# Attention sink weights: turned in two halves on VectorE and through DRAM instead of on TensorE, with the values of two head pairs multiplied in mid-attention

## The chip, the cores and the metric

The kernel runs on one NeuronCore of one Trainium2 chip. The metric is the device time of one execution in microseconds (us). Three executions were timed, and one more was profiled. In the profile PE is the matrix engine (TensorE) and PEld its weight loads; DVE is VectorE, ACT is ScalarE, POOL is GpSimd, and SP is the engine whose queue issues most transfers here.

## The reference

A banded attention with sink keys feeds a two-layer feed-forward network with a PReLU in the middle. The shapes are batch 4, 8 heads, 768 positions, head size 64, a window of 128 keys, 4 sink keys; then 3072 rows, model width 512, inner width 2048.

```python
scores = scale * np.matmul(q, k.transpose(0, 1, 3, 2))
is_sink = pos[None, :] < int(n_sink)
in_window = (rel >= 0) & (rel < int(window))
scores = np.where(is_sink | in_window, scores, -1000000000.0)
a = np.exp(scores - np.max(scores, axis=-1, keepdims=True))
a = a / (np.sum(a, axis=-1, keepdims=True) + 1e-09)
attn_out = np.matmul(a, v)
x = attn_out.transpose(0, 2, 1, 3).reshape(B * S, H * D)
h = x @ w_in
g = np.maximum(h, 0.0) + alpha * np.minimum(h, 0.0)
out = g @ w_out
```

## The kernel before

The 3072 rows are worked in 12 chunks of 256 positions (`NCHUNK`), three to each batch. The attention of chunk c+1 runs beside the feed-forward network of chunk c. The network of a chunk has 16 slots (`NF`), one for each block of 128 inner columns: `gemm1` (12 matmuls, 256 columns wide), then the PReLU on ACT and DVE with a split into a high and a low part, and two slots later `gemm2` (6 matmuls, 512 columns wide, in two pieces). All products of the network are made from such high and low parts.

The attention of a chunk from 2 on takes 8 heads one after another. For each head and each half of the 256 positions there is a pair of score matmuls (L591, L592), the mask and the row minimum on DVE (L604), the exponential on ACT (L608). `finish_head` makes the reciprocals on DVE (L637, L638), the scaled weights of the window (L649, into a tile named comb), and on POOL the scaled weights of the four sink keys (L653, into the tile sink). The weights must then be turned, so that keys lie on partitions. From chunk 3 on (`PAIRED`) the window's weights of each head pair go this way in `swap`: DVE turns 32 by 32 blocks (L713), SP sends the tile to a DRAM scratch named swap (L716), and four transfers bring it back with the blocks in their turned places (L719). In `swapped` DVE multiplies them by triangles into a tile named wa (L730). The sink weights of all heads of a chunk are handled once, in `sink_step`: two DVE instructions split them into a high and a low part (L678, L679, tile ts), two PE transposes turn them (L684), and ACT copies them to sinkT (L687). `av_two` takes two head pairs at a time. It opens two PSUM banks with a matmul each of the sink weights (L816), adds the window's values (24 narrow matmuls at L746), and ACT and DVE split the result into xh and xl (L826, L827), which `gemm1` of the next chunk reads.

The order is not that of the code. A planner (`Plan.draw`) simulates the five engines with a cost for each operation and a rule for transfers, and picks at every point the operation that can start, by its rank. PE's operations are ranked in the order in which the program creates them, those of the others just ahead of the first that needs them. What the planner drew is then issued in that order on each engine, with real semaphore waits. `attention` gives the steps of a chunk as a list, and `spread` deals the 26 steps out over 12 of the 16 slots. In the planner a PE operation may start 0.5 us after an input from another engine is due:

```python
SLACK = 0.5
...
dma = max(dma, t + 1.5) + o.nbytes / 290e3
end = dma + 0.5
```

Tiles come from small pools: comb has 4, swap 2, sinkT 1, the PSUM kind pa 2, stage (raw queries and keys) 2, v 2.

Of the kernel before, what the change touches and what calls it, by code (L numbers as in the profile page):

```python
# [9 lines left out]
F32 = mybir.dt.float32  # L10
# [9 lines left out]
P = 128  # L20
# [300 lines left out]
def program(ctx, tc, qk, pairs, vp, vs, w, par, out):  # L321
# [12 lines left out]
    def several(name, n, shape, dtype):  # L334
        plan.kind(name, [pool.tile(shape, dtype, name=f"{name}{i}") for i in range(n)])

    scratch = ctx.enter_context(tc.tile_pool(name="scratch", bufs=1, space=bass.MemoryType.DRAM))
    plan.kind("swap", [scratch.tile([4, P, P], F32, name=f"swap{i}") for i in range(2)])
    several("stage", 2, [P, QC + KC], F32)
    several("kq", 2, [P, KC + 2 * QC], F32R)  # L340
    several("v", 2, [P, 3, 2, D], F32)
# [318 lines left out]

    def sink_step(c, g=0):
        sm, sk = sums[c], sink[c]
        heads = range(4 * g, 4 * g + 4) if c in SPLIT else range(H)
        if c in SPLIT:
            r, wide = val("ri"), val("ob")
            rinv[c, g] = wide
            four = lambda: r.at.rearrange("p (h u) -> p h u", u=2)
            op("DVE", 0.15, lambda: nc.vector.tensor_scalar(four(), sm.at[:, 4 * g:4 * g + 4], 1e-9, None, op0=ALU.add),
               reads=[(sm, (h, u)) for h in heads for u in range(2)], writes=[r])
            op("DVE", 0.16, lambda: nc.vector.reciprocal(four(), four()), writes=[r])  # L670
            each = lambda: r.at.rearrange("p (h u) -> p u h", u=2).unsqueeze(3).broadcast_to([P, 2, 4, D])
            fold = lambda: wide.at.rearrange("p (u h d) -> p u h d", u=2, h=4)
            op("ACT", cast(8 * D), lambda: nc.scalar.copy(fold(), each()), reads=[r], writes=[wide],
               other=("DVE", dve(8 * D, True), lambda: nc.vector.tensor_copy(fold(), each())))
        sp = lambda: sk.at.rearrange("p u h s -> p u (h s)").unsqueeze(2).broadcast_to([P, 2, 2, 32])
        ts, tp = val("ts"), val("pa")
        done = [(sk, h) for h in range(heads[-1] + 1)]
        op("DVE", 0.14, lambda: nc.vector.tensor_copy(ts.at[:, :, 0::2], sp()), reads=done, writes=[(ts, 0)])  # L678
        op("DVE", 0.2, lambda: nc.vector.tensor_tensor(ts.at[:, :, 1::2], sp(), ts.at[:, :, 0::2].bitcast(F32), ALU.subtract),  # L679
           reads=done + [(ts, 0)], writes=[(ts, 1)])  # L680

        def turn():
            for u in range(2):
                nc.tensor.transpose(tp.at[:, u * P:(u + 1) * P], ts.at[:, u].rearrange("p a x -> p (a x)").bitcast(F32), ident)  # L684
        op("PE", 2 * TURN, turn, reads=[ts], writes=[tp], tail=T_TAIL)
        st = sinkT[c] = val("sinkT")
        op("ACT", cast(QC, True), lambda: nc.scalar.copy(st.at, tp.at[:, :QC]), reads=[tp], writes=[st])  # L687
# [120 lines left out]
    def av_two(c, p):  # L808
        both = (p, p + 1)
        src, v = [wt.pop((c, x)) for x in both], [vtile.pop((c, x)) for x in both]  # L810
        bks = [val("pa") for _ in both]
        vt, st = vst[c // CPB], sinkT[c]

        def sinks():
            for bk, x in zip(bks, both):
                nc.tensor.matmul(bk.at[:, :QC], vt.at[:, x * P:(x + 1) * P], st.at, start=True, stop=False)  # L816
        op("PE", 2 * mm(QC), sinks, reads=[vt, st], writes=bks, tail=R_TAIL)
        x1, x2 = begin_x(c, p)

        def both_values():  # L820
            for n in range(2):
                values(c, v[n].at, lambda j: src[n].at.bitcast(F32)[:, j * 4 * P:(j + 1) * 4 * P], bks[n].at[:, :QC])
        op("PE", 2 * values_cost(c), both_values, reads=src + v, writes=bks, tail=N_TAIL, mode="col")
        for n, x in enumerate(both):
            a = bks[n]
            op("ACT", cast(QC, True), lambda a=a, x=x: nc.scalar.copy(x1.at[:, x], a.at[:, :QC]), reads=[a], writes=[(x1, x)])  # L826
            op("DVE", dve(QC), lambda a=a, x=x: nc.vector.tensor_tensor(x2.at[:, x], a.at[:, :QC], x1.at[:, x].bitcast(F32), ALU.subtract),  # L827
               reads=[a, (x1, x)], writes=[(x2, x)])
            if p + 2 < KT:
                load_v(c, x + 2)  # L830
# [65 lines left out]
    def attention(c):  # L896
        def a_step(h, u):
            def run():
# [5 lines left out]
                unit(c, h, u)  # L904
                if u == 1:
                    finish_head(c, h)
                    if h in (5, 6):
                        load_v(c, h - 5)
            return run

        def b_steps(pairs):
# [6 lines left out]
        if c in SPLIT:  # L918
# [16 lines left out]
                steps.insert(at, st)  # L935
            return steps
        steps = [a_step(h, u) for h in range(H) for u in range(2)]
        steps += [None, sk]
        if c >= PAIRED:
            for p in (0, 2):  # L940
                steps += [lambda p=p: trans(c, p), lambda p=p: trans(c, p + 1), None, lambda p=p: av_two(c, p)]
            return steps
        b = b_steps(range(KT))
        for n, st in enumerate(b):
            steps.append(st)
# [272 lines left out]
```

## Time and profile before

| quantity | value |
| --- | --- |
| median of the three timed executions | 679.52 us (679.45 to 680.26) |
| time of the profiled execution | 680.06 us |
| its span from the first to the last instruction | 678.4 us |
| PE busy in the span | 665.8 us (98%) |
| DVE busy | 522.7 us (77%) |
| ACT busy | 407.2 us (60%) |
| POOL busy | 31.7 us (5%) |
| mean granted TensorE clock | 0.997 of full speed |

The span leaves out what lies around the instructions. Matmuls are pipelined, so the duration of one in the trace is longer than the step to the next, and what a matmul costs PE is read from one start to the next start.

### The profile page before, as it was taken

The numbers are of one execution on the slowest core, as the hardware profiler recorded it, in microseconds if no ns is written. First come the engines' busy times: TensorE is split into PE (matmuls) and PEld (weight loads), VectorE is DVE, ScalarE is ACT, GpSimd is POOL, SyncE is SP. The second block draws the span as 40 slices with busy tenths as digits, with TensorE's granted clock in tenths as the row PEclk, the third lists the DMA queues.
The fourth block names the chain that finished last, engine by engine and source line by source line (L and its number), as shares of the span: only waits on it lengthen the run. The fifth ranks groups of instructions, "written<-read, shape, count | busy, mean of one in ns | idle before, by whom it ended". The sixth has DMA issues, their size and how long they took to land.

```text
span 678.4 us, 13475 instructions
## 1 busy us (share of the span) xinstructions
PE 665.8 (98%) x4552; PEld 582.2 (86%) x4552; DVE 522.7 (77%) x1759; ACT 407.2 (60%) x1093; POOL 31.7 (5%) x115
## 2 busy tenths in 40 slices
PE   9989999999999999999999999999999999999996
PEld 4568898988889989988988988988988988988995
DVE  6999999967967976976885985985895994895331
ACT  6989987837627636736735735744753852852432
POOL 2110000001000000010000000000000000000000
PEclk9989999999999999999999999999999999999999
DMA  8765541325342533443442542542442443322001
GB/s 312 270 217 212 189 164 46 120 79 149 102 118 91 142 106 115 136 126 95 126 141 77 143 125 82 155 134 71 137 119 81 143 115 104 115 74 71 32 2 36
DMA packets 67901, 82.60 MB, mean 122 GB/s; under 512 B 5872, under 2 KB 48880, under 8 KB 67824
## 3 DMA queue, kind: packets, MB, share of 16 engines
q1 hardware_dynamic: 64272, 68.55, 34.1%
q10 hardware_dynamic: 3552, 13.11, 5.6%
q8 instruction: 38, 0.62, 0.4%
q14 instruction: 39, 0.32, 0.1%
HBM read 65.91 MB, written 15.73 MB: 120 GB/s over the span
## 4 chain that ended last, share of the span: by engine, by line
PE 82%; DVE 9%; ACT 5%; issue 1%; DMA 1%; POOL 0%; SPq 0%; ACTq 0%; DVEq 0%
PE bank L841 34%; PE bank L878 12%; PE bank L876 11%; PE bank L879 11%; PE bank L746 5%; PE bank L591 3%; PE bank L592 3%; DVE wa L393 2%; DVE w L401 2%; ACT pt L608 1%; ACT wa L379 1%; DVE wa L391 1%; DVE gl L848 1%; PE bank L1031 1%; DVE g L846 1%
## 5 line engine op out<-in xcount | busy, mean ns | idle before, releaser
L841 PE MATMUL bank<-xh,w 128*128 128x256 f32 x1536 | 307.7, 281 | 1.7 <-DVE g L846 1.5
L841 PEld LDWEIGHTS bank<-xh,w 128*128 128x128 f32 x1536 | 251.0, 189 | 10.6 <-DVE g L846 3.4
L841 PE MATMUL bank<-xl,w 128*128 128x256 f32 x768 | 214.8, 280 | 0.0
L845 ACT ACTIVATE g<-bank,param 128x256 f32<-128x256 f32 x192 | 90.5, 473 | 131.4 <-PE bank L841 128.8
L878 PE MATMUL bank<-w,gh 128*128 128x512 f32 x382 | 153.1, 401 | 0.0
L879 PE MATMUL bank<-w,gh 128*128 128x512 f32 x382 | 149.9, 392 | 0.0
L841 PEld LDWEIGHTS bank<-xl,w 128*128 128x128 f32 x768 | 145.2, 189 | 5.3
L846 DVE TENSOR_TENSOR g<-bank,g 128x256 f32<-128x256 f32 x192 | 80.1, 419 | 58.2 <-ACT g L845 57.4
L876 PE MATMUL bank<-w,gl 128*128 128x512 f32 x382 | 119.9, 395 | 0.0
L847 ACT CAST gh<-g 128x256 fp32r<-128x256 f32 x192 | 77.1, 404 | 66.8 <-DVE g L846 65.8
L608 ACT ACTIVATE pt<-pt,nm 128x260 f32<-128x260 f32 (+1 forms) x192 | 94.0, 490 | 17.7 <-DVE nm L604 17.1
L848 DVE TENSOR_TENSOR gl<-g,gh 128x256 fp32r<-128x256 f32 x192 | 81.1, 424 | 30.2 <-ACT gh L847 27.6
L876 PEld LDWEIGHTS bank<-w,gl 128*128 128x128 f32 x382 | 69.7, 188 | 14.5 <-issue 0.7
L604 DVE CUSTOM_DVE_ANT_0 pt<-bank,masks 128x260 f32<-128x260 f32 (+1 forms) x192 | 73.9, 400 | 8.5 <-PE bank L592 5.5
L878 PEld LDWEIGHTS bank<-w,gh 128*128 128x128 f32 x382 | 71.9, 188 | 9.9 <-issue 1.5
L879 PEld LDWEIGHTS bank<-w,gh 128*128 128x128 f32 x382 | 71.9, 188 | 8.3
L730 DVE TENSOR_TENSOR wa<-comb,tri 128x256 f32<-128x256 f32 x144 | 52.4, 419 | 12.4 <-DMA comb<-swap 12.2
L557 DVE TENSOR_TENSOR kq<-stage,kq 64x392 fp32r<-64x392 f32 x80 | 45.3, 566 | 10.7 <-ACT kq L555 8.7
L555 ACT CAST kq<-stage 128x392 fp32r<-128x392 f32 x80 | 41.5, 519 | 10.6 <-PE bank L592 7.3
L592 PE MATMUL bank<-kq 128*128 128x260 f32 (+1 forms) x160 | 44.5, 281 | 0.0
L591 PE MATMUL bank<-kq 128*128 128x260 f32 (+1 forms) x160 | 44.0, 279 | 0.1
L649 DVE CUSTOM_DVE_ANT_0 comb<-pt,ri 128x128 f32<-128x128 f32 x136 | 43.1, 346 | 0.0
(125 smaller groups left out, 657.4 us busy)
## 6 DMA issues: line engine op xcount, KB each, us to landing
stage<-qk SPq DMA_DIRECT2D x80, 324.0 KB, 2.9
wraw<-w ACTq DMA_DIRECT2D x12, 1024.0 KB, 5.2
swap<-comb SPq DMA_DIRECT2D x36, 256.0 KB, 2.2
comb<-swap SPq DMA_DIRECT2D x144, 64.0 KB, 2.1
v<-vp SPq DMA_DIRECT2D x44, 192.0 KB, 2.9
out_dram<-ob SPq DMA_DIRECT2D x22, 256.0 KB, 2.2
wraw<-w SPq DMA_DIRECT2D x4, 1024.0 KB, 11.3
lent<-pairs SPq DMA_DIRECT2D x4, 324.0 KB, 4.5
```

The source lines that it names most:

```text
L591: nc.tensor.matmul(s[:, w0], qh()[:, qs], ks()[:, kw], start=True, stop=False)
L592: nc.tensor.matmul(s[:, w0], ql()[:, qs], ks()[:, kw], start=False, stop=True)
L604: op("DVE", dve(n), lambda: nc.vector.tensor_tensor_reduce(out=pt.at[:, u, w0], in0=s.at[:, w0], in1=masks[:, i, w0], scale=-0.125, scalar ...
L608: op("ACT", exp(n), lambda: nc.scalar.activation(pt.at[:, u, w0], pt.at[:, u, w0], AF.Exp, bias=nm.at[:, h, u:u + 1], scale=-1.0, accum_ou ...
L841: nc.tensor.matmul(h(), fin.at[:, 0, part, ks], rhs.at[:, kt], start=(kt == 0 and n == 0), stop=(kt == KT - 1 and n == 2))
L845: op("ACT", act(QC, True), lambda: nc.scalar.activation(g.at, h(), AF.Copy, scale=alt[:, f:f + 1]), reads=[bk, known("param")], writes=[g])
L846: op("DVE", dve(QC), lambda: nc.vector.tensor_tensor(g.at, h(), g.at, ALU.max), reads=[bk], writes=[g])
L847: op("ACT", cast(QC), lambda: nc.scalar.copy(gh.at, g.at), reads=[g], writes=[gh])
L848: op("DVE", dve(QC), lambda: nc.vector.tensor_tensor(gl.at, g.at, gh.at.bitcast(F32), ALU.subtract), reads=[g, gh], writes=[gl])
L876: nc.tensor.matmul(o2[j].at, gl.at[:, js], fin.at[:, 1, 0], start=False, stop=(f == NF - 1))
L878: nc.tensor.matmul(o2[j].at, gh.at[:, js], fin.at[:, 1, 0], start=(f == 0), stop=False)
L879: nc.tensor.matmul(o2[j].at, gh.at[:, js], fin.at[:, 1, 1], start=False, stop=False)
```

## The change

For chunks 3 to 11 `sink_step` now runs twice, for heads 0 to 3 and for heads 4 to 7. Each time both DVE instructions handle the columns of all heads as before. In place of the two PE transposes and the ACT copy, DVE turns 32 by 32 blocks into a comb tile (L686 of the new file), SP sends them to a DRAM scratch named turns (L688), and four transfers bring them to sinkT (L691). The blocks in sinkT lie in another order, and the matmuls of the sink weights (L831) read them through a view with runs of 32 elements. The steps of `attention` are put in another order: the first half of the sink weights after head 3, the first two head pairs' values a few steps later, and heads 4 to 7 around and after them. The loads of v for pairs 0 and 1 are issued after heads 1 and 2 in place of 5 and 6.

```diff
--- before.py
+++ after.py
@@ -336,6 +336,7 @@
 
     scratch = ctx.enter_context(tc.tile_pool(name="scratch", bufs=1, space=bass.MemoryType.DRAM))
     plan.kind("swap", [scratch.tile([4, P, P], F32, name=f"swap{i}") for i in range(2)])
+    plan.kind("turns", [scratch.tile([4, P, 2 * 32], F32, name=f"turns{i}") for i in range(2)])
     several("stage", 2, [P, QC + KC], F32)
     several("kq", 2, [P, KC + 2 * QC], F32R)
     several("v", 2, [P, 3, 2, D], F32)
@@ -660,7 +661,7 @@
 
     def sink_step(c, g=0):
         sm, sk = sums[c], sink[c]
-        heads = range(4 * g, 4 * g + 4) if c in SPLIT else range(H)
+        heads = range(4 * g, 4 * g + 4) if c in SPLIT or c >= PAIRED else range(H)
         if c in SPLIT:
             r, wide = val("ri"), val("ob")
             rinv[c, g] = wide
@@ -673,11 +674,25 @@
             op("ACT", cast(8 * D), lambda: nc.scalar.copy(fold(), each()), reads=[r], writes=[wide],
                other=("DVE", dve(8 * D, True), lambda: nc.vector.tensor_copy(fold(), each())))
         sp = lambda: sk.at.rearrange("p u h s -> p u (h s)").unsqueeze(2).broadcast_to([P, 2, 2, 32])
-        ts, tp = val("ts"), val("pa")
+        ts = val("ts")
         done = [(sk, h) for h in range(heads[-1] + 1)]
         op("DVE", 0.14, lambda: nc.vector.tensor_copy(ts.at[:, :, 0::2], sp()), reads=done, writes=[(ts, 0)])
         op("DVE", 0.2, lambda: nc.vector.tensor_tensor(ts.at[:, :, 1::2], sp(), ts.at[:, :, 0::2].bitcast(F32), ALU.subtract),
            reads=done + [(ts, 0)], writes=[(ts, 1)])
+
+        if c >= PAIRED:
+            small, d = val("comb"), val("turns")
+            st = sinkT[c] = val("sinkT")
+            op("DVE", dve(QC), lambda: nc.vector.transpose(
+                small.at[:, :QC].rearrange("p (j u b) -> p u j b", u=2, j=4), ts.at.bitcast(F32)), reads=[ts], writes=[small])
+            op("SP", ISSUE, lambda: nc.sync.dma_start(d.at.rearrange("j p x -> p j x"), small.at[:, :QC].rearrange("p (j x) -> p j x", j=4)),
+               reads=[small], writes=[d], nbytes=4 * P * QC)
+            for j in range(4):
+                op("SP", ISSUE, lambda j=j: nc.sync.dma_start(
+                    st.at[j * 32:(j + 1) * 32].bitcast(F32).rearrange("a (i x) -> a i x", i=4), d.at[j].rearrange("(i a) x -> a i x", i=4)),
+                   reads=[d], writes=[(st, j)], nbytes=4 * 32 * QC)
+            return
+        tp = val("pa")
 
         def turn():
             for u in range(2):
@@ -813,7 +828,7 @@
 
         def sinks():
             for bk, x in zip(bks, both):
-                nc.tensor.matmul(bk.at[:, :QC], vt.at[:, x * P:(x + 1) * P], st.at, start=True, stop=False)
+                nc.tensor.matmul(bk.at[:, :QC], vt.at[:, x * P:(x + 1) * P], st.at.rearrange("p (i u b) -> p u i b", u=2, i=4), start=True, stop=False)
         op("PE", 2 * mm(QC), sinks, reads=[vt, st], writes=bks, tail=R_TAIL)
         x1, x2 = begin_x(c, p)
 
@@ -904,8 +919,9 @@
                 unit(c, h, u)
                 if u == 1:
                     finish_head(c, h)
-                    if h in (5, 6):
-                        load_v(c, h - 5)
+                    first = 1 if c >= PAIRED else 5
+                    if h in (first, first + 1):
+                        load_v(c, h - first)
             return run
 
         def b_steps(pairs):
@@ -935,11 +951,12 @@
                 steps.insert(at, st)
             return steps
         steps = [a_step(h, u) for h in range(H) for u in range(2)]
+        if c >= PAIRED:
+            for p, n in ((2, 16), (0, 8)):
+                steps[n:n] = [lambda p=p: sk(p // 2)]
+                steps[n + 3:n + 3] = [lambda p=p: trans(c, p), lambda p=p: trans(c, p + 1), None, lambda p=p: av_two(c, p)]
+            return steps
         steps += [None, sk]
-        if c >= PAIRED:
-            for p in (0, 2):
-                steps += [lambda p=p: trans(c, p), lambda p=p: trans(c, p + 1), None, lambda p=p: av_two(c, p)]
-            return steps
         b = b_steps(range(KT))
         for n, st in enumerate(b):
             steps.append(st)
```

Line numbers of the new file differ: L604 became L605, L637 and L638 became L638 and L639, L649 became L650, L678 and L679 became L679 and L680, L713, L716 and L719 of `swap` became L728, L731 and L734, L730 became L745, L746 became L761, L816 became L831, L841, L846 and L848 became L856, L861 and L863, L876 to L879 became L891 to L894, L438 became L439, L453 became L454, L557 and L559 became L558 and L560.

First PE, in chunk 4's attention, where the first two head pairs are multiplied. The tile ts holds the split sink weights, wa the turned window weights, w8 to w12 the network's weights, gh and gl its split activations. Before:

```order
L841 MATMUL bank5_69<-xh1_110,w11_942 128x256
L684 MATMUL bank3_67<-ident_129,ts0_104 128x128 x2
L878 MATMUL bank6_70<-w9_859,gh0_115 128x512
L879 MATMUL bank6_70<-w9_859,gh0_115 128x512
L878 MATMUL bank7_71<-w9_859,gh0_115 128x512
L879 MATMUL bank7_71<-w9_859,gh0_115 128x512
L876 MATMUL bank6_70<-w9_859,gl0_118 128x512
L876 MATMUL bank7_71<-w9_859,gl0_118 128x512
L816 MATMUL bank2_66<-sinkT0_105,vs0_106 128x256
L816 MATMUL bank3_67<-sinkT0_105,vs0_106 128x256
L746 MATMUL bank2_66<-wa0_89,v0_80 64x256 x2
L746 MATMUL bank2_66<-wa0_89,v0_80 64x128 x4
```

Now:

```order
L894 MATMUL bank7_71<-w8_810,gh2_119 128x512
L831 MATMUL bank2_66<-sinkT0_107,vs0_108 128x256
L831 MATMUL bank3_67<-sinkT0_107,vs0_108 128x256
L761 MATMUL bank2_66<-wa0_91,v0_82 64x256 x2
L761 MATMUL bank2_66<-wa0_91,v0_82 64x128 x4
L761 MATMUL bank3_67<-wa1_92,v1_83 64x256 x2
L761 MATMUL bank3_67<-wa1_92,v1_83 64x128 x4
L891 MATMUL bank6_70<-w8_810,gl2_122 128x512
L891 MATMUL bank7_71<-w8_810,gl2_122 128x512
L592 MATMUL bank1_65<-kq1_81 128x260
L593 MATMUL bank1_65<-kq1_81 128x260
```

The transposes L684 are gone. The matmuls of the sink weights and the values stand between the two pieces of the `gemm2` of block 8, where before they stood behind that of block 9; and the last score pair of head 7 (kq1) follows them, where before all scores of the chunk were ahead of them.

Next SP's queue in the second half of chunk 4's attention; stage is loaded from qk, v from vp. Before:

```order
L716 DMA swap0_74<-comb1_86 128x4x128
L438 DMA stage1_77<-qk 128x648
L453 DMA v0_80<-vp 128x384
L719 DMA comb3_88<-swap0_74 32x4x128 x4
L453 DMA v1_81<-vp 128x384
L716 DMA swap1_75<-comb0_85 128x4x128
L719 DMA comb1_86<-swap1_75 32x4x128 x4
L453 DMA v0_80<-vp 128x384
L453 DMA v1_81<-vp 128x384
```

Now:

```order
L731 DMA swap0_74<-comb1_88 128x4x128
L454 DMA v0_82<-vp 128x384
L454 DMA v1_83<-vp 128x384
L439 DMA stage0_78<-qk 128x648
L734 DMA comb0_87<-swap0_74 32x4x128 x4
L731 DMA swap1_75<-comb3_90 128x4x128
L439 DMA stage1_79<-qk 128x648
L734 DMA comb1_88<-swap1_75 32x4x128 x2
L688 DMA turns1_77<-comb2_89 128x4x64
L734 DMA comb1_88<-swap1_75 32x4x128 x2
L691 DMA sinkT0_107<-turns1_77 32x4x64 x4
```

The transfer to turns stands between the second and the third of the four that bring back the last head pair's weights, and the four to sinkT follow them.

Last DVE in the same stretch, from the sink weights' split on. Before:

```order
L637 TENSOR_SCALAR ri3_100<-sm0_95 128x2
L638 RECIPROCAL ri3_100<-ri3_100 128x2
L846 TENSOR_TENSOR g0_113<-bank4_68,g0_113 128x256
L678 CAST ts0_104<-sink0_91 128x4x32
L679 TENSOR_TENSOR ts0_104<-sink0_91,ts0_104 128x4x32
L730 TENSOR_TENSOR wa1_90<-comb2_87,tri_130 128x256 x4
L848 TENSOR_TENSOR gl1_119<-g0_113,gh1_116 128x256
L713 STREAM_TRANSPOSE comb1_86<-comb0_85 128x4x4x32
```

Now (from the last L650 on; the split L679 and L680 stands just ahead of the four L650 of this head pair):

```order
L650 ISA comb2_89,jk0_103<-pt_0_84,ri3_102 128x128
L650 ISA jk0_103 128x1
L728 STREAM_TRANSPOSE comb3_90<-comb2_89 128x4x4x32
L863 TENSOR_TENSOR gl2_122<-g1_116,gh2_119 128x256
L861 TENSOR_TENSOR g0_115<-bank4_68,g0_115 128x256
L560 TENSOR_TENSOR kq1_81<-stage1_79,kq1_81 128x256
L745 TENSOR_TENSOR wa0_91<-comb0_87,tri_132 128x256 x4
L863 TENSOR_TENSOR gl0_120<-g0_115,gh0_117 128x256
L861 TENSOR_TENSOR g1_116<-bank5_69,g1_116 128x256
L686 STREAM_TRANSPOSE comb2_89<-ts0_106 128x2x4x32
```

The block transposition of the sink weights, L686, waits in the order behind the triangles of pair 2 (L745) and a PReLU (L861), and uses the comb tile that the last L728 has just read.

## Rows read from the trace of the kernel before

**Rows 1.** The page's part 1: busy time, share of the span, instructions.

```profile
PE 665.8 (98%) x4552; PEld 582.2 (86%) x4552; DVE 522.7 (77%) x1759; ACT 407.2 (60%) x1093; POOL 31.7 (5%) x115
```

**Rows 2.** Busy time of each engine in stretches of the span, two of thirteen.

```profile
core 0: us, PE busy (x) PEld busy (x) DVE busy (x) ACT busy (x) POOL busy (x), PEclk, DMA share, GB/s
...
158.00:212.00 54.00, 53.72 (x367) 47.84 (x366) 39.52 (x142) 29.33 (x86) 1.63 (x7) 1.00 0.37 104
...
423.00:476.00 53.00, 53.00 (x377) 47.69 (x376) 42.09 (x156) 31.23 (x90) 3.33 (x9) 1.00 0.43 121
```

**Rows 3.** Timeline of PE in and behind chunk 4's attention: start, duration, engine, line, operation.

```profile
237.78 0.38 PE L684 MATMUL bank<-ident,ts 128*128 128x128 f32 x2
...
238.24 0.39 PE L879 MATMUL bank<-w,gh 128*128 128x512 f32 x1
...
250.25 0.28 PE L841 MATMUL bank<-xh,w 128*128 128x256 f32 x1
...
251.64 0.39 PE L878 MATMUL bank<-w,gh 128*128 128x512 f32 x1
251.87 0.39 PE L879 MATMUL bank<-w,gh 128*128 128x512 f32 x1
...
253.01 0.28 PE L841 MATMUL bank<-xh,w 128*128 128x256 f32 x1
...
259.26 0.28 PE L591 MATMUL bank<-kq 128*128 128x260 f32 x1
259.38 0.28 PE L592 MATMUL bank<-kq 128*128 128x260 f32 x1
```

**Rows 4.** Timeline of DVE in chunk 4's attention, the same columns.

```profile
235.22 0.34 DVE L649 CUSTOM_DVE_ANT_0 comb<-pt,ri 128x128 f32<-128x128 f32 x1
...
235.52 0.17 DVE L637 TENSOR_SCALAR ri<-sm 128x2 f32<-128x2 f32 x1
...
235.87 0.42 DVE L846 TENSOR_TENSOR g<-bank,g 128x256 f32<-128x256 f32 x1
236.26 0.23 DVE L678 CAST ts<-sink 128x128 fp32r<-128x128 f32 x1
...
236.74 1.42 DVE L730 TENSOR_TENSOR wa<-comb,tri 128x256 f32<-128x256 f32 x4
238.08 0.41 DVE L848 TENSOR_TENSOR gl<-g,gh 128x256 fp32r<-128x256 f32 x1
238.41 0.70 DVE L713 STREAM_TRANSPOSE comb<-comb 128x512 f32<-128x512 f32 x1
239.04 0.38 DVE L846 TENSOR_TENSOR g<-bank,g 128x256 f32<-128x256 f32 x1
239.45 0.56 DVE L557 TENSOR_TENSOR kq<-stage,kq 64x392 fp32r<-64x392 f32 x1
240.03 0.43 DVE L848 TENSOR_TENSOR gl<-g,gh 128x256 fp32r<-128x256 f32 x1
```

**Rows 5.** Timeline of SP's queue over chunks 3 to 11: the issues of transfers.

```profile
327.67 0.38 SPq L716 DMA_DIRECT2D swap<-comb  x1
...
329.89 1.75 SPq L719 DMA_DIRECT2D comb<-swap  x4
...
400.45 1.80 SPq L719 DMA_DIRECT2D comb<-swap  x4
...
455.65 0.43 SPq L716 DMA_DIRECT2D swap<-comb  x1
459.21 1.74 SPq L719 DMA_DIRECT2D comb<-swap  x4
...
509.56 1.75 SPq L719 DMA_DIRECT2D comb<-swap  x4
```

**Rows 6.** Timeline of DVE: the shortest and longest way back from DRAM.

```profile
404.87 1.43 DVE L730 TENSOR_TENSOR wa<-comb,tri 128x256 f32<-128x256 f32 x4 [1.24 <-DMA comb<-swap]
...
512.87 1.43 DVE L730 TENSOR_TENSOR wa<-comb,tri 128x256 f32<-128x256 f32 x4 [0.71 <-DMA comb<-swap]
```

## Prediction

> **What bounds the kernel now.** I read the page's first part first. PE is busy for 665.8 of 678.4 us and DVE for 77% [rows 1]. A busy PE alone proves little, so I read the stretches next: from the fourth chunk on a stretch of 53 us holds 53.00 us of PE work, DVE has 42.09 us in it, and the clock is granted in full; in the stretch before, where the first changed chunk's attention runs, PE lacks 0.28 of 54 us [rows 2]. So PE sets the time of the nine changed chunks, and there are hardly any waits to take away. Whatever leaves PE's instruction stream leaves the time; whatever makes PE wait is added. What an instruction costs PE is the step from its start to the next start, since matmuls overlap.
>
> **What leaves PE.** Each changed chunk loses two transposes, 18 in all. In chunk 4 the pair starts at 237.78 and the second matmul of the `gemm2` behind it at 238.24, 0.46 us later. Without a pair ahead of it the first of these starts at 251.64 and the second at 251.87, 0.23 us later [rows 3]. A pair therefore costs 0.46 - 0.23 = 0.23 us, and nine cost 2.1 us. The nine ACT copies to sinkT and nine uses of a PSUM bank go too; ACT is busy for 31.23 of 53 us [rows 2], so I count nothing for them. The matmuls of the sink weights and the two bursts of values per chunk stay, with the same changes of tile shape around them.
>
> The Trainium skill bears on this trade. Its page "VectorE: DVE Perf Modes", section "Rules for kernel authors", says to turn a 128 by 128 block on TensorE where a PSUM destination is acceptable, which speaks against the change; the section "The three transpose paths" gives 390 ns for one there. By that figure 18 of them would be worth an estimated 7.0 us. The trace shows 0.23 us for two in this stream, so the sum goes by 2.1 us.
>
> **What is added to DVE.** Nine more casts and subtractions of the split, 0.87 - 0.39 = 0.48 us a pair (L846 starts at 235.87, L678 at 236.26, L730 at 236.74), and 18 block transpositions of 256 columns. The trace has those of 512 columns at 0.63 us from start to start [rows 4]; half of that is 0.3 and the whole is the upper bound, and I take 0.35 us, near the half. This is 0.48 + 2 x 0.35 = 1.2 us a chunk, which brings DVE from 42.1 to 43.3 of 53 us [rows 2]. Eleven us of work in all lie beside PE as long as DVE's share stays below PE's; if that cover went, each of them would be on the path. The scores are spread over more slots than before, so DVE is not pressed harder in the busy slots, and I count nothing.
>
> **What is added to SP and the transfers.** 18 transfers out and 72 back, at 0.44 us of issue each by the four that take 1.75 us [rows 5]: 40 us on a queue that mostly waits. They stand in order on it, and that matters: the transfer of the turned sink weights stands behind the way out of the chunk half's second head pair and two of its four returns, and two returns and the four to sinkT stand behind it. The loads of stage and v also queue there, but they are needed a head or more later.
>
> **The new wait, priced.** PE used to get the sink weights through its own transposes and a copy. Now the first matmul on sinkT waits for a second round trip to DRAM behind the first. In PE's order the values follow these matmuls at once in all 18 places, so everything behind them on PE waits too. I work out how long PE has before it gets there, and how long the chain takes.
>
> In chunk 4's second half PE runs, between the last scores of head 7 and the sink weights, 66 matmuls of `gemm1` and 34 of `gemm2`. Twelve of the first kind take 251.64 - 250.25 = 1.39 us and six of the second 253.01 - 251.64 = 1.37 [rows 3], so PE arrives after 7.65 + 7.76 = 15.4 us. In the first half there are, from head 3's last scores on, 72 and 34 and 14 score matmuls at 0.12 (259.26 and 259.38): 8.34 + 7.76 + 1.68 = 17.8 us.
>
> The chain in the second half begins on DVE. In its order, from the mask of head 7 to the end of the last window transposition, stand four instructions of about 256 columns (mask, two halves of xl, a PReLU) at 0.33 to 0.41, say 0.35; a key split at 0.58 (239.45 to 240.03); the reciprocals at 0.35 (235.52 to 235.87); the split of the sink weights, 0.48; four weighted tiles at 0.30 (235.22 to 235.52); the transposition, 0.63 [rows 4]. That is 1.4 + 0.58 + 0.35 + 0.48 + 1.2 + 0.63 = 4.6, and I add 0.2 for PE's end, an estimate: 4.8 us. In the first half the same count gives 6.8 us.
>
> From there a common tail follows. The way out until the first return is issued took from 2.22 us (327.67 to 329.89) to 3.56 us (455.65 to 459.21), and two returns take half of 1.75 [rows 5]. This is 3.1 to 4.4 us. Meanwhile DVE must get to the turn of the sink weights: three PReLU or split instructions and a query split behind the transposition, four triangles (236.74 to 238.08) and one more PReLU, 5 x 0.35 + 1.34 = 3.1 us, and the turn itself 0.35 [rows 4]: 3.5 us, so the tail's first part is 3.5 to 4.4. No row shows the way out and back of the turned sink weights; they move half the bytes in as many pieces. I bound them by the rows of the window's weights: out 2.2 to 3.6 us, back from 3.31 us (first issue at 509.56, use at 512.87) to 4.42 us (400.45 to 404.87) [rows 5, 6]. The tail is 9.0 to 12.4 us. With the middles 2.7, 3.7 and 3.9, the first a little under its ends' mean because half the bytes move, I take 10.3 us.
>
> So the sink weights are due 4.8 + 10.3 = 15.1 us after head 7's scores where PE arrives at 15.4, and 17.1 us after head 3's where it arrives at 17.8. They come just in time, with 0.3 and 0.7 us to spare; by the short ends 1.6 and 2.0 us are left, by the long ends PE waits 1.8 and 1.4 us. In the likeliest case a wait shows in a few of the 18 places, and I charge 0.3 us in all. **The sum** for the profiled execution is 678.4 - 2.1 + 0.3 = 676.6 us of span. Its own time was 680.06, which becomes 678.3; the median stands 0.5 us below that execution, so it becomes 679.52 - 1.8 = 677.7 us.
>
> **The rivals.** *The sink weights come late.* This one ends slower. Its place is the first matmul on sinkT, 18 times. By the long ends the price is 9 x (1.8 + 1.4) = 28.8 us; an average lateness of 0.12 us at each place uses up the 2.1 us, and 0.2 us makes the kernel slower by more than can be overlooked. At 0.4 us it would be 679.5 - 2.1 + 7.2 = 684.6 us. For it speaks that both margins are smaller than the spread of one transfer; against it that the ends would have to be long several times in one chain. The skill's page "DMA: Bandwidth & Descriptors", section "Specifications", says that pieces under 512 bytes are moved by read and modify, below line rate, and the pieces here are 256 bytes. By that rule the halved bytes bring nothing, the tail lies nearer its long end, and this rival gains; no row of the trace shows it.
>
> *A few waits eat the gain.* The same mechanism at an average of 0.08 us a place: 18 x 0.08 = 1.4 us of 2.1, and 678.8 us, not to be told from no change.
>
> *The view with runs of 32 elements slows the matmuls of the sink weights.* If their step doubled, each pair would cost 2 x 0.116 = 0.23 us more [rows 3], 18 pairs 4.2 us: 681.6 us. All moving operands of the old program are read in one run, so the trace neither shows nor excludes it.
>
> *DVE becomes the bound.* It would have to be late for a PReLU by more than the two slots between `gemm1` and `gemm2`; with 43.3 of 53 us it is not. A tenth of its 11 us on the path would give 678.5 us.
>
> **How the numbers follow.** A difference under 0.2%, 1.36 us, can't be told from no change here. The forecast has a chance of 0.52, the few waits 0.21, late sink weights 0.18, the view 0.05, DVE 0.04. Faster by more than 0.2% is the forecast alone, 0.52; within 0.2% are the few waits and DVE, 0.25; slower are the late weights and the view, 0.23. The likeliest case's own range is 676.9 to 678.2 us. The range reaches below that for a wait of the old kernel that goes with the change (0.28 us in rows 2) and a pair of transposes worth a little more, to 676.8, and above to the middle of the late case, 683.5.
>
> **What would show it.** In the changed profile: no matmul from ts but those of chunks 0 to 2; PE full in the stretches of chunks 4 to 10, which are shorter by 0.2 us a chunk; no wait of PE for a transfer from turns to sinkT. The prediction is wrong if the waits of PE list sinkT at most of its 18 places, if the step of the matmuls on sinkT is above 0.12 us, or if PE waits for a PReLU in the slots where heads 4 to 7 now stand.

## The result, and the profile after

The changed kernel took 682.40 us in the median of 12 executions (680.09 to 683.42) where the kernel before took 679.51 us (12 executions, 678.76 to 681.01): a ratio of 1.0037, 95% interval 1.0027 to 1.0048. It is slower by 0.37%; 677.7 us was forecast. Its profiled execution took 681.54 us, with a span of 679.8 us, 1.4 us more than before. The medians are 2.9 us apart and the profiled executions 1.5 us; what follows accounts for the profiled ones, and no trace shows the other 1.4 us. In one later run (e8_own_tile_late2) one of six executions took 812.91 us at a granted clock of 0.752, and its median below is that of the other five.

Part 1 of the changed kernel's page shows what was meant to happen: PE has 1.3 us less to do than in [rows 1], DVE 6.4 us more (11 were counted).

```profile
PE 664.5 (98%) x4532; PEld 581.1 (85%) x4534; DVE 529.1 (78%) x1795; ACT 401.9 (59%) x1084; POOL 35.1 (5%) x115
```

The waits of PE in the changed kernel (engine, line, operand, releaser: us in total, times, longest us) begin with a line that the kernel before could not have:

```profile
PE bank L831 <- DMA sinkT<-turns: 3.0, 4, 1.4
```

L831 is the matmul of the sink weights. In stretches of the changed kernel (length, then busy time of PE, PEld, DVE, ACT and POOL, the granted clock, the transfers' share and rate), PE lacks 0.74, 0.84 and 1.38 us in chunks 3 to 5, and nothing from 317 us on; in [rows 2] 0.28 us was missing in the first.

```profile
158.00:212.00 54.00, 53.26 (x363) 47.59 (x362) 39.81 (x141) 28.44 (x82) 1.67 (x7) 1.00 0.40 112
212.00:264.00 52.00, 51.16 (x361) 45.54 (x361) 40.60 (x155) 27.83 (x81) 2.27 (x8) 1.00 0.42 118
264.00:317.00 53.00, 51.62 (x360) 45.89 (x358) 41.40 (x156) 28.46 (x84) 3.52 (x9) 1.00 0.47 131
317.00:370.00 53.00, 53.00 (x367) 47.74 (x367) 42.82 (x154) 30.68 (x89) 2.43 (x8) 1.00 0.45 126
```

By starts, the step into the first matmul of a pair on sinkT is 0.91, 0.62, 0.54 and 1.53 us too long at 181.33, 236.47, 255.59 and 310.08 us and right at the other 14 places: 3.6 us of wait against 2.1 us of transposes.

The largest, in the second half of chunk 5, can be followed through three timelines of the changed kernel. PE's has the last scores of head 7 and the sink weights:

```profile
292.95 0.28 PE L593 MATMUL bank<-kq 128*128 128x260 f32 x1
...
310.08 0.47 PE L831 MATMUL bank<-sinkT,vs 128*128 128x256 f32 x2 [1.38 <-DMA sinkT<-turns]
```

DVE's has the triangles of the first half's second head pair, ahead of which DVE stood idle for 1.58 us, the second half's transposition, its triangles and the turn:

```profile
288.59 1.44 DVE L745 TENSOR_TENSOR wa<-comb,tri 128x256 f32<-128x256 f32 x4 [1.58 <-DMA comb<-swap]
...
299.59 0.71 DVE L728 STREAM_TRANSPOSE comb<-comb 128x512 f32<-128x512 f32 x1
...
301.32 1.44 DVE L745 TENSOR_TENSOR wa<-comb,tri 128x256 f32<-128x256 f32 x4
...
303.34 0.44 DVE L686 STREAM_TRANSPOSE comb<-ts 128x256 f32<-128x256 f32 x1
```

SP's queue has both halves:

```profile
282.34 0.79 SPq L734 DMA_DIRECT2D comb<-swap  x2
283.82 0.38 SPq L688 DMA_DIRECT2D turns<-comb  x1
284.25 0.99 SPq L734 DMA_DIRECT2D comb<-swap  x2
...
303.81 0.38 SPq L688 DMA_DIRECT2D turns<-comb  x1
304.24 1.82 SPq L734 DMA_DIRECT2D comb<-swap  x2
306.94 1.73 SPq L691 DMA_DIRECT2D sinkT<-turns  x4
```

Two links are to be seen. In the first half the way out of the turned sink weights (283.82) holds back two of the four returns (284.25), so DVE idles until 288.59 and reaches the second half late: its transposition ends 7.3 us after head 7's scores. Then the way out of 303.81 needs 3.13 us until the first return can be issued, against 1.93 us at the quickest places, and the sink weights land 17.1 us after the scores, where PE arrived after 15.6.

### The profile page after: what moved, and what is told of

Its sections match the earlier page's. It is cut to its first block, busy times and chain, and to the rows that moved or that the text cites. A ratio compares the mean times of both kernels' runs of the same rounds, so it can differ in the third digit from the quotient of the medians.

```text
span 679.8 us, 13577 instructions
## 1 busy us (share of the span) xinstructions
PE 664.5 (98%) x4532; PEld 581.1 (85%) x4534; DVE 529.1 (78%) x1795; ACT 401.9 (59%) x1084; POOL 35.1 (5%) x115
## 4 chain that ended last, share of the span: by engine, by line
PE 77%; DVE 9%; DMA 5%; ACT 4%; issue 2%; SPq 1%; POOL 0%; ACTq 0%; DVEq 0%; POOLq 0%
PE bank L856 33%; PE bank L891 11%; PE bank L893 11%; PE bank L894 10%; PE bank L761 5%; PE bank L592 2%; PE bank L593 2%; DMA comb<-swap 2%; DVE wa L745 1%; ACT pt L609 1%; DMA turns<-comb 1%; DVE wa L394 1%; DMA sinkT<-turns 1%; DVE g L861 1%; ACT wa L380 1%
## 5 line engine op out<-in xcount | busy, mean ns | idle before, releaser
L856 PE MATMUL bank<-xh,w 128*128 128x256 f32 x1536 | 306.4, 281 | 1.4 <-DVE g L861 1.2
L856 PEld LDWEIGHTS bank<-xh,w 128*128 128x128 f32 x1536 | 250.7, 189 | 9.1 <-DVE g L861 2.5
L856 PE MATMUL bank<-xl,w 128*128 128x256 f32 x768 | 214.9, 280 | 0.0
L894 PE MATMUL bank<-w,gh 128*128 128x512 f32 x382 | 149.8, 392 | 0.0
L856 PEld LDWEIGHTS bank<-xl,w 128*128 128x128 f32 x768 | 145.1, 189 | 5.2
L891 PE MATMUL bank<-w,gl 128*128 128x512 f32 x382 | 120.8, 397 | 0.0
L861 DVE TENSOR_TENSOR g<-bank,g 128x256 f32<-128x256 f32 x192 | 79.6, 416 | 46.8 <-ACT g L860 45.9
L863 DVE TENSOR_TENSOR gl<-g,gh 128x256 fp32r<-128x256 f32 x192 | 80.5, 420 | 20.1 <-ACT gh L862 17.6
L891 PEld LDWEIGHTS bank<-w,gl 128*128 128x128 f32 x382 | 69.0, 188 | 15.7 <-issue 2.7
L605 DVE CUSTOM_DVE_ANT_0 pt<-bank,masks 128x260 f32<-128x260 f32 (+1 forms) x192 | 73.6, 400 | 10.7 <-PE bank L593 8.0
L894 PEld LDWEIGHTS bank<-w,gh 128*128 128x128 f32 x382 | 71.9, 188 | 8.3
L745 DVE TENSOR_TENSOR wa<-comb,tri 128x256 f32<-128x256 f32 x144 | 51.5, 420 | 20.6 <-DMA comb<-swap 20.0
L558 DVE TENSOR_TENSOR kq<-stage,kq 64x392 fp32r<-64x392 f32 x80 | 45.2, 565 | 7.8 <-ACT kq L556 5.2
L654 POOL TENSOR_TENSOR sink<-pt,ri 128x8 f32<-128x8 f32 x80 | 21.9, 276 | 504.1 <-DVE ri L639 289.3
```

Of the source, the lines that this page charges most:

```text
L605: op("DVE", dve(n), lambda: nc.vector.tensor_tensor_reduce(out=pt.at[:, u, w0], in0=s.at[:, w0], in1=masks[:, i, w0], scale=-0.125, scalar ...
L745: op("DVE", dve(2 * P), lambda j=j, u=u: nc.vector.tensor_tensor(full()[:, j, u].rearrange("p l (i b) -> p l i b", i=4), view()[:, j, u].u ...
L856: nc.tensor.matmul(h(), fin.at[:, 0, part, ks], rhs.at[:, kt], start=(kt == 0 and n == 0), stop=(kt == KT - 1 and n == 2))
L861: op("DVE", dve(QC), lambda: nc.vector.tensor_tensor(g.at, h(), g.at, ALU.max), reads=[bk], writes=[g])
L863: op("DVE", dve(QC), lambda: nc.vector.tensor_tensor(gl.at, g.at, gh.at.bitcast(F32), ALU.subtract), reads=[g, gh], writes=[gl])
L891: nc.tensor.matmul(o2[j].at, gl.at[:, js], fin.at[:, 1, 0], start=False, stop=(f == NF - 1))
```

## The experiments

Each ran beside the kernel before on the same chip: e1 to e4 on one chip, e5 to e9 on a second, e10, e11 and e0 on a third, e12 and e13 on a fourth. Which chip the first measurement had is not on record. The part of the program before chunk 3's attention is the same in all, but takes up to 2.5 us more in one execution than in another (last section). So beside the medians the table gives, of each profiled execution, the time from the start of the 384th matmul of `gemm1` to that of the 2,304th, the last, counted in the trace, as "changed part", and the sum of the too long steps into the first sink-weight matmul as "wait". The kernel before has 526.53 us there.

| run | median, us | ratio to before | changed part, us | wait, us |
| --- | --- | --- | --- | --- |
| changed kernel | 682.40 | 1.0037 [1.0027, 1.0048] | 528.18 | 3.6 |
| e1_no_sink_read | 677.68 | 0.9984 [0.9972, 0.9995] | 524.01 | 0 |
| e2_order_only | 682.38 | 1.0046 [1.0032, 1.0060] | 528.57 | - |
| e3_turn_only | 699.13 | 1.0289 [1.0270, 1.0308] | 544.82 | 9.3 |
| e4_planned_later | 684.01 | 1.0068 [1.0054, 1.0082] | 531.54 | 0.2 |
| e5_own_tile | 681.05 | 1.0028 [1.0015, 1.0040] | 528.05 | 0.9 |
| e8_own_tile_late1 | 683.34 | 1.0046 [1.0034, 1.0059] | 528.79 | 1.0 |
| e8_own_tile_late2 | 681.56 | 1.0033 [1.0020, 1.0045] | 527.28 | 0 |
| e9_wide_out | 681.19 | 1.0019 [1.0010, 1.0029] | 527.24 | 3.0 |
| e10_turn_earlier | 677.28 | 0.9966 [0.9953, 0.9979] | 524.01 | 0 |
| e11_turn_later | 679.50 | 0.9995 [0.9984, 1.0007] | 524.71 | 0.4 |
| e0_changed_again | 679.55 | 1.0003 [0.9988, 1.0017] | 526.45 | 2.1 |
| e12_changed_third | 680.27 | 1.0005 [0.9993, 1.0018] | 525.86 | 1.7 |
| e13_earlier_again | 678.28 | 0.9969 [0.9958, 0.9981] | 523.99 | 0 |

In the runs that were planned anew (e3, and both e8) "wait" is what the list of waits has for that line.

**The wait taken away by other data.**

```diff
-                nc.tensor.matmul(bk..., st.at.rearrange("p (i u b) -> p u i b", u=2, i=4), ...)
+                nc.tensor.matmul(bk..., vt.at[:, :QC].rearrange("p (i u b) -> p u i b", u=2, i=4), ...)
```

> The changed kernel with one operand exchanged: the matmuls of the sink weights read the head pair's value tile, with the same view of runs of 32 elements, in place of sinkT, so the product of the sink weights of chunks 3 to 11 is left out and PE has no wait for the turned sink weights; the split, the turn and all its transfers stay, in the same order. Theory A, the wait: what makes the changed kernel slower is PE's wait for the transfers into sinkT. Then all of it goes: no wait in front of these matmuls, the 2.1 us of the 18 transposes show, and the time is 679.5 - 2.1 = 677.4 us. Theory B, the load: VectorE's and SyncE's added work or the moved values cost the time. Then it stays at 682 us. Theory C, the view: it stays at 682 us too, with a step of these matmuls above 0.12 us.

677.68 us, and PE is full in chunks 3 to 5 with all added work in place. So the wait is what costs, and theories B and C fall. The account closes step by step: PE's order is that of the changed kernel, and of the 4.17 us between the two changed parts 3.97 us are in the steps into the matmuls of the sink weights. The view with runs of 32 elements costs nothing: the two matmuls of a pair are 0.118 us apart.

```profile
212.00:264.00 52.00, 52.00 (x367) 46.76 (x366) 41.89 (x157) 29.04 (x85) 2.26 (x8) 1.00 0.43 123
264.00:317.00 53.00, 53.00 (x374) 47.56 (x373) 42.42 (x160) 30.00 (x88) 3.52 (x9) 1.00 0.45 130
```

**The order alone.** The block `if c >= PAIRED: ... return` of `sink_step` is taken out again, so TensorE's turn follows, twice a chunk.

> The new order of steps alone (sink weights in two halves, values of two head pairs in mid-attention), the turn done by TensorE and copied by ScalarE as before the change, so twice a chunk: 36 transposes where the kernel before has 18. Theory A: the order is harmless and no matmul waits; the time is 679.5 + 2.1 = 681.6 us from the 18 added transposes, at 0.23 us a pair, with every stretch of TensorE full. Theory B, the order itself makes TensorE wait: 681.6 us and some 3 to 5 us more, about 686 us, with idle time in TensorE at PReLU or weights in the stretches from chunk 3 on.

The changed part is 528.57 - 526.53 = 2.04 us longer, for 18 transposes more: 2.1 us was the estimate. PE is full in every stretch from 158 us on. The order is harmless, and 18 transposes are worth some 2.1 us of the time. The median is 0.8 us above the 681.6 expected; only the changed part, of one execution, shows the 2.04.

**The turn alone.** `sink_step` once for all heads and the values behind attention, as before.

> The turn through DRAM alone, once a chunk for all heads, with the values after attention as before the change: 9 turns, 36 returns. Its place leaves TensorE some 17 to 23 us of work between the last scores and the sink weights, where the changed kernel has 15 to 17. Theory A, the wait: TensorE comes later than the sink weights at most places; the 18 transposes leave and little waits, 677.5 us (677.2 to 679). Theory B, the round trip itself is what costs, by its load on the queues: half of it is left, so about half of the loss against 677.4 us stays, 680 us.

A miss by 21 us. PE waits at L831 four times, in a chunk's second burst of values, with the sink weights in place for over 5 us (last issue 199.66, matmul 207.42); the list of waits names DVE's `xl`, by which a PSUM bank of the first burst comes free.

```profile
PE bank L831 <- DVE xl L842: 9.3, 4, 2.8
PE bank L856 <- DVE g L861: 3.0, 7, 0.7
```

The granted clock adds to it: it was 0.50, or 1.2 GHz, from 208.6 to 212.0 us, just behind a wait of 2.66 us, and from 536.3 to 543.1, from the last part of one of 2.81 us on. The first of the two stretches (columns as above, the clock third from the end):

```profile
208.61:212.02 3.41, 3.41 (x20) 2.62 (x21) 3.03 (x17) 1.41 (x5) 0.50 (x2) 0.50 0.31 97
```

The 10.2 us at half the clock are an estimated 5.1 us lost, and PE is idle for 13.1 us from 158 to 635 us; that is 18.2 of the 20.8 us by which the changed part is longer than e1's. The rest stays open. The planner made another program of it, and it tells nothing of the changed kernel's wait.

**Planned later.** A number `late` is added to the transfers of the turn in the planner.

```diff
-                end = dma + 0.5
+                end = dma + 0.5 + o.late
```

> The changed kernel, with one number of the planner: it counts each transfer of the turn 0.75 us longer, and so puts the sink weights' matmuls 0.4 to 2.6 us of TensorE's work later in the order. Nothing else is changed on purpose. Theory A, the wait: an average lateness of some 0.3 us a place is covered at nearly all places; waits in front of the sink weights under 1 us in all, 677.5 to 678.3 us. Theory B, the load: the same work stays, 682 us. Theory C, the view: 682 us.

The wait for sinkT is gone but for 0.2 us, and the kernel is slower still. Here PE waits for DVE, which itself stood at the triangles; in the DVE timeline and the PE timeline of this run (all lines one higher):

```profile
565.55 1.43 DVE L746 TENSOR_TENSOR wa<-comb,tri 128x256 f32<-128x256 f32 x4 [2.46 <-DMA comb<-swap]
566.90 0.75 DVE L864 TENSOR_TENSOR gl<-g,gh 128x256 fp32r<-128x256 f32 x2
```

```profile
567.37 0.74 PE L892 MATMUL bank<-w,gl 128*128 128x512 f32 x2 [1.79 <-DVE gl L864]
```

DVE waits in order for a return of the swap, two `gl` stand behind it, and a `gemm2` on PE behind these. Behind this wait the granted clock was 0.50 from 568.8 to 572.2 us, an estimated 1.7 us more. A larger cost in the planner moved the wait to another place.

**A tile of its own, with the planner free.** `small` from the kind rb in place of comb; the two e8 runs add `late=0.75` and `late=1.5`.

> The changed kernel, but VectorE's turned sink weights go into a tile of their own and not into one of the four comb tiles, so that the turn no longer stands behind the second head pair's swap; the planner then puts the sink weights' matmuls 4 to 6 us of TensorE's work earlier (11 us behind the scores of heads 3 and 7, was 15 to 18). Theory A, the wait: what counts is the chain against the place. The chain gets some 4 to 5 us shorter and the place moves by as much, so lateness is about as in the changed kernel or more: 681 to 686 us, with waits on sinkT at most places. Theory B, the place behind the swap is itself the cause: waits on sinkT vanish, 677.5 us.

> The tile of its own, and the planner counts each transfer of the turn 0.75 us longer: the sink weights' matmuls stand 12 to 13 us behind the scores, the values 14.5 us behind those of head 7. Theory A, the wait: 1.1 to 1.4 us more than in the run with the tile of its own alone; its waits on sinkT shrink by up to that at each place, to about 679 to 681 us, if the order brings no other wait. Theory B, an earlier order of any kind costs: no change against that run.

> The same with 1.5 us more for each transfer: 13.5 to 15.1 us behind the scores, with a chain that is some 4 us shorter than the changed kernel's. Theory A, the wait: the sink weights are there at all 18 places, no wait on sinkT; the 18 transposes show and the time is 677.5 us (677.0 to 679.5, the upper end for VectorE's waits on the swap's returns that the values bring). Theory B, the load: 682 us.

The waits on sinkT shrink to 0.9, 1.0 and 0 us (not at most places, as expected of the first), but none of the three comes near 677.5 us. All were ordered anew, and the changed part is 3.3 to 4.8 us longer than in e1. Idle time of PE in chunks 3 to 11 explains only 1.5, 2.7 and 0.5 us of it. Some 1.1 us in e5 and e8_own_tile_late2 is in the second score matmul, which starts 0.119 us behind the first in the mean and not 0.111 (144 of them). The rest stays open. Theory A holds for the wait and fails for the time: an order that the planner makes afresh brings other losses. Times near 682 us do not speak for the load either, since e1 carries all of it at 677.68 us.

**The way out twice as wide.** turns is `[4, P, P]`, and all 512 columns of the comb tile go out.

> The changed kernel in its very order, with the way out of the turned sink weights twice as wide: pieces of 512 bytes where there were 256, so 256 KB in place of 128 KB; half of what is written is never read back. The Trainium skill's page DMA: Bandwidth & Descriptors, section Specifications, says that pieces under 512 bytes cost a read and a modify; by that rule the wider pieces land no later, and the waits stay or shrink: 680.5 to 682.4 us. Rival: what a landing takes goes by the bytes, as the window's weights with the same pieces do in the changed kernel's transfers (2.2 us in the median beside 2.0 us): each of the four or more late places waits 0.2 to 0.5 us longer, 683 to 684.5 us.

The way out took 2.2 us in the median beside 2.0 us, from issue to landing, in the groups of transfers of this run and of the changed kernel (operands, issues, KB each, us):

```profile
turns<-comb SPq DMA_DIRECT2D x18, 256.0 KB, 2.2
```

```profile
turns<-comb SPq DMA_DIRECT2D x18, 128.0 KB, 2.0
```

At the quick places the first return is issued 2.24 us after the way out, before 1.93 us. So the wider pieces landed later, not sooner. In the traces a packet of 256 bytes took 18 ns in the median and one of 512 bytes 27 ns. The smaller piece is dearer by the byte, but it isn't the cost that the prediction and this run's expectation made of the rule on the Trainium skill's page "DMA: Bandwidth & Descriptors", section "Specifications". The time, 681.19 us, is as the rule would have it, but lies within what the changed kernel itself varies by; it decides nothing.

**The turn moved, the order kept.** In both runs the planner's list is made as in the changed kernel, and then entries are moved in it.

```diff
+    early = lambda what, e: [x for x in steps if getattr(x[0], "early", None) == what and x[1] == e]
+    for e in ("DVE", "SP"):
+        for x, y in zip(early("swap", e), early("turn", e)):
+            steps.remove(y)
+            steps.insert(steps.index(x) + 1, y)
     plan.issue(steps, fill, WARM)
```

Here `"turn"` marks L686 and L688, and `"swap"` the transposition and the way out of pairs 1 and 3; the turned blocks go to the idle tile rb. In e11 only L688 moves, behind the last return. PE's order in both traces is that of the changed kernel.

> The order of TensorE and ScalarE is that of the changed kernel, row by row. On VectorE the turn of the sink weights is moved ahead of the triangles, right behind the second pair's block transposition, into a tile that lies idle since the first chunks, and on SyncE its way out right behind that pair's way out. The way out then starts some 1.5 us behind the transposition's start, where it was 4.0 to 5.7 us, and the returns to sinkT are held back only by the four returns of the swap. Theory A, the wait: the sink weights land 0.5 to 2.3 us sooner, most at the late places, where 0.5 to 1.5 us were missing; no wait on sinkT is left, and the time is that of the run without the read, 677.7 us (677.2 to 678.5). Theory B, the new work or the order costs the time: 682 us, since both stay.

> The order of TensorE, ScalarE and VectorE is that of the changed kernel, row by row; on SyncE alone the turn's way out stands behind all four returns of the second pair, where two of them stood behind it at many places. The way out starts up to 1 us later there (two issues at 0.44 us). Theory A, the wait: 0.4 to 1 us more is missing at the late places and some of the places that were in time by less than that become late: 684 to 688 us. Theory B: what costs the time is not this wait; 682 us as in the changed kernel, or less, since the swap's returns come sooner.

The first came out as theory A had it: 677.28 us, faster than both kernels, PE full in every stretch from 158 us on. The same half of chunk 5 in this run, in the timelines of DVE, SP and PE:

```profile
295.09 0.71 DVE L728 STREAM_TRANSPOSE comb<-comb 128x512 f32<-128x512 f32 x1
295.73 0.40 DVE L686 STREAM_TRANSPOSE rb<-ts 128x256 f32<-128x256 f32 x1
```

```profile
295.83 0.38 SPq L731 DMA_DIRECT2D swap<-comb  x1
296.31 0.45 SPq L688 DMA_DIRECT2D turns<-rb  x1
...
298.08 1.74 SPq L734 DMA_DIRECT2D comb<-swap  x4
299.92 2.63 SPq L691 DMA_DIRECT2D sinkT<-turns  x4
```

```profile
290.45 0.28 PE L593 MATMUL bank<-kq 128*128 128x260 f32 x1
...
306.04 0.40 PE L831 MATMUL bank<-sinkT,vs 128*128 128x256 f32 x2
```

The transposition now ends 5.3 us after the scores, where it was 7.3, and the last return is issued 11.7 us after them, in place of 15.3.

The second was a miss that taught the first link. Its way out came up to 0.7 us later behind the transposition at most places (4.8 us in chunk 5's second half, where it was 4.2), and yet the wait fell to 0.4 us. The reason is on DVE. Its lines of waits for the swap's returns (us, times, longest) are, in the changed kernel's first trace, in its second (e0, on the same chip as the two runs that move the turn), in e11 and in e10:

```profile
DVE wa L745 <- DMA comb<-swap: 20.0, 20, 2.3
```

```profile
DVE wa L745 <- DMA comb<-swap: 12.3, 16, 1.9
```

```profile
DVE wa L745 <- DMA comb<-swap: 3.6, 9, 0.7
```

```profile
DVE wa L745 <- DMA comb<-swap: 2.5, 5, 0.7
```

With no turn between the returns DVE is held up far less, and ends the transposition in chunk 5's second half 5.5 us after the scores. The wait ahead of it, 1.58 us at 288.59 in the changed kernel, was 1.36 and 1.30 us in its other two traces (e0, e12), and is gone in e11 and e10. The sums say less: before the change it was 12.2 us in 12 places, as much as in e0. In time e11 brought nothing against the changed kernel on the same chip (679.50 and 679.55 us), though its changed part is 1.7 us shorter. Its profiled execution lost 1.9 us ahead of the changed part, with the clock (last section); whether the others did is not shown.

**How large the loss is.**

> The changed kernel once more, beside the two runs that move its turn: 682.4 us, between 681.5 and 683.3.

> The changed kernel a third time, since its first measurement gave 682.4 us and its second 679.55 us. If the loss goes by how long the transfers take on a chip, it lies anywhere between these two, and the profiled execution shows as much more span from the 384th matmul of gemm1 to the last (528.2 and 526.5 us so far) as its waits on sinkT are longer (3.6 and 2.1 us). If one of the two was a stray, it falls within 0.5 us of the other.

> The kernel with the turn moved ahead, once more beside the changed kernel. Theory A, the wait: with no wait on sinkT left it doesn't share the spread of the changed kernel: 677.3 us again (676.8 to 678.0), wherever the changed kernel comes out.

The first of these was a miss by 2.9 us: in both later measurements the changed kernel is not to be told from the kernel before. PE's waits for sinkT are, in e0 and in e12:

```profile
PE bank L831 <- DMA sinkT<-turns: 1.5, 2, 1.1
```

```profile
PE bank L831 <- DMA sinkT<-turns: 1.4, 2, 1.2
```

By starts they are 2.1 and 1.7 us, with all late places in chunks 3 to 5 and the largest in chunk 5's second half each time. The changed part follows the wait: 528.18, 526.45 and 525.86 us for 3.6, 2.1 and 1.7. The version without the wait came out at 678.28 us, 0.3 above its range, on a chip where the kernel before took 679.87; its ratios are 0.9966 and 0.9969. So the loss of 0.37% holds for the first measurement; over all three the change brings no gain, since the wait takes what the transposes give. Why the transfers took longer in one measurement than in another stays open: the runs don't separate the chip from the execution.

## Why the prediction was wrong, step by step

**What bounds the kernel** was right: what leaves PE's stream shows as soon as PE doesn't wait. **The 2.1 us** of the transposes were right, 2.04 by e2, or 0.11 us for one; the 390 ns that the prediction names from the Trainium skill's page "VectorE: DVE Perf Modes", section "The three transpose paths", stand there for a bf16 block. In e1 and e10 2.5 us of the changed part go; most of the surplus of 0.4 us is the wait of 0.28 us in [rows 2], which is gone there and which the prediction allowed for in its range.

**PE's arrival** was right: 15.4 and 17.8 us after the scores were forecast, and the trace of the changed kernel has 15.6 and 18.0 at 13 of 18 places (15.5 in chunk 3's first half, 17.9 and 18.6 in chunks 6 and 9). **The tail** was right in size: 10.3 us taken, 9.0 to 12.4 as bounds; from the end of the transposition to 1.86 us behind the last issue to sinkT (the landing for which PE waited in chunk 4's first half and chunk 5's second) the trace has 8.6 to 11.2 us, 9.7 in the mean, and one landing was 1.5 us longer. One of its terms was taken too short: 3.7 us stands in the sum as the middle of 3.5 to 4.4, which is 3.95, and by that the margins would have been 0.05 and 0.45 us.

**The charge of 0.3 us** for the new wait is the step that failed: the wait was 3.6 us. These 3.3 us are about the whole miss of the profiled execution (678.3 us forecast, 681.54 measured); of the 4.7 us by which the median was missed, 1.4 are in no trace. The rival "the sink weights come late" held, with 0.2 us a place in the mean of 18. Two things were wrong in the charge. The margins of 0.3 and 0.7 us were compared as if they were the same at each place. But a late place costs and an early one gives nothing back, so the price is the sum over late places alone: with margins from -1.5 to over 2 us their mean says little, and 4 of 18 cost 3.6 us. The prediction had the spread in its own ends (2.0 us to spare to 1.8 us of wait) and priced only the middle.

And **the start of the chain**, 4.8 us after head 7's scores and 6.8 after head 3's, took DVE's work without its waits. The trace has 4.5 to 7.3 us at the places where PE arrives after 15.6, and 7.4 in the first halves from chunk 4 on. The prediction named what stands behind the turn on SP ("two returns and the four to sinkT") but followed only the sink weights, not who waits for those two returns. That is DVE, in order, with the next half's work behind it; so DVE's added waits were not nothing. e10, which takes the turn out from between the returns, shows it: 5.3 us in place of 7.3 in chunk 5's second half, 5.7 in place of 6.4 in chunk 4's. At the other two late places the start was no later than in e10; there the tail was long, 11.2 us in chunk 4's first half and 11.6 in chunk 3's.

**The other rivals** fell: the view (0.118 us a matmul) and DVE as the bound (PE full in e1 with DVE at 42 of 53 us). DVE's own part in the turn cost nothing in e1 and e10. The Trainium skill's page "VectorE: DVE Perf Modes", section "Rules for kernel authors", would leave such a turn on TensorE; this case agrees only as long as PE waits for the turn, and e10 gains 0.34% with it on DVE.

## What to carry to other kernels

A wait at many places is priced as the sum of the late ones, over the spread of both sides, never as the difference of two means. A transfer set into a queue in order is followed to everyone behind it: here to an engine whose delay came back as the next lateness of the same transfer. And a wait is tested, and cured, with the order held: the four runs of the changed kernel's steps that let the planner place the sink weights anew were 3 to 8 us above e1 in the changed part, and the two that moved a few entries of a fixed list at most 0.7 us.

## What the runs showed of the hardware

The part ahead of chunk 3 is one program in all runs, and yet the 384th matmul of `gemm1` starts between 140.8 and 143.3 us. The granted clock goes with it. It was 0.50, or 1.2 GHz, for 6.8 us in e2 (start at 143.20) and for 3.4 us in the changed kernel (141.50), in the stretches

```profile
37.60:44.42 6.82, 6.05 (x27) 4.99 (x25) 6.24 (x20) 6.35 (x17) 1.75 (x4) 0.50 0.43 145
```

```profile
38.98:42.40 3.42, 3.42 (x17) 3.13 (x16) 3.39 (x8) 3.42 (x13) 0.61 (x2) 0.50 0.36 100
```

Half of the 3.4 us between them is the 1.70 us between the two starts. All fifteen traces fit: no such stretch in e5 (start at 140.8), 3.4 us of it in nine (141.4 to 141.9), 6.8 us in five (142.7 to 143.3). From 26 to 40 us PE is busy for 11.5 to 11.6 of 14 us in e5, the changed kernel and e2 alike, so why the stretch is longer in some is not shown.

This is as large as the effect under study, so single executions were compared by the changed part alone. And one transfer of 128 KB took from 1.9 to 3.6 us until the return that waits for it could be issued, at 18 like places of one execution.
